# Block-recurrent attention and an ELU feed-forward on one core: batch 0 laid out as one hand-written order over all engines

## The chip, the cores and the metric

The kernel runs on one core of a Trainium2 chip. The metric is the device time of one execution in microseconds (us). Three runs of the kernel before gave 882.35 (median), 882.07 and 882.54 us.

A core has five engines that take instructions from queues of their own, in order, and hand results over by semaphores: PE (TensorE, matrix products and transposes), DVE (VectorE), ACT (ScalarE), POOL (GpSimd) and SP (SyncE, which here only issues DMAs). PEld is the loading of weights into PE.

## The reference, cut to what matters

Eight batches of 512 tokens; 8 heads of 64; each batch has 32 state rows per head.

```python
# x (8, 8, 512, 64) float32, state (8, 8, 32, 64) float32
# w_in (512, 2048), w_out (2048, 512): float64
scores = scale * x @ state.T                       # per batch and head
xread = softmax(scores) @ state                    # tokens read states
sread = softmax(scale * state @ x.T) @ x           # states read tokens
y = concat([xread, sread], axis=2)                 # (8, 8, 544, 64)
x = y.transpose(0, 2, 1, 3).reshape(8 * 544, 512)
h = x @ w_in
g = where(h > 0, h, exp(minimum(h, 0)) - 1)        # ELU
out = g @ w_out                                    # (4352, 512) float32
```

The softmaxes run over the last axis. Both weights arrive as float64, as pairs of 32-bit words, and the kernel makes float32 of them itself.

## The kernel before

**Batch by batch.** For each batch of 512 tokens the kernel does the attention, then 16 tiles of the hidden layer (`ffn1`, tile name `h_ps`, 128 hidden units by 512 tokens each) with the ELU on each, then the output layer (`ffn2`, `o_ps`) in four chunks of 128 tokens, each a sum over the 16 tiles. `xread` is never formed: `make_m` multiplies the transposed states (`kT`) with a quarter of `w_in` (512 columns) into `m_ps`, copied to `m_sb`, and `ffn1` multiplies that with the transposed attention weights `aT`. The state rows of all batches (`xT_state`) go through both layers at the end.

**Attention of a batch.** `turn_x` transposes x on PE in two halves (`xT_ps`), ACT copies them out; `by_state` gives the scores (`s_ps`, rows of 4 heads by 32 states; two halves g = 0, 1). `softmaxes` does both softmaxes for a half: over tokens by DVE (maximum, L221) and ACT (exp with sum, L229), over states by a 32x32 transpose on DVE (L226), maximum (L235), subtraction on POOL (L236), exp on ACT (L237), sum (L245), reciprocal and a multiplication on POOL (L250). `turn_tokens` transposes back to `aT` on DVE (L255), `turn_state` transposes `a_s` on PE, `state_read` computes `sr_ps`.

**The weights.** 32 pieces of 128x512: 16 of `w_in` (four column quarters of four pieces) and 16 of `w_out`. `load_weights` issues a transfer of 512 KB from SP into one of seven buffers named `raw`; `convert` turns the float64 words into float32 with three instructions on ACT (L150, L153, L156) and four on DVE (L157, L163, L167, L171). A buffer is free for the next transfer when the last of these has read it.

**ELU (`elu`).** ACT takes exp of `h_ps` into `e_sb` (L297), DVE limits it to 1 (L298), and DVE takes max(e - 1, h) into `g_sb` (L300).

**What sets the order.** PE's instructions stay in the order in which the code is written. Those of the other engines are put in order by a scheduler, which follows the order of the code loosely and mixes independent steps. In batch 0 the code is: states and x loaded, first quarter of `w_in` converted, attention of batch 0, the first `m`, then the 16 hidden tiles, with one more piece of weights converted after each; then all remaining pieces (`more(len(rest))`), and only then the output layer. From batch 1 on, the attention of the next batch is hooked in between the matmuls of the output layer, every fourth one, and the next `m` before the last chunk.

**PSUM.** `ps_a` is one buffer of two banks for all transposes, scores, `m_ps` and `sr_ps`; `ps_h` has three banks for `h_ps`; `ps_o` three for `o_ps`.

Of the kernel before, what the change touches and what calls it, by code (L numbers as in the profile page):

```python
# [25 lines left out]
def kernel(  # L26
# [23 lines left out]
    NB = S // 32  # L50
    scale = 1.0 / math.sqrt(D)
# [20 lines left out]
    rawpool = pool("raw", 7)  # L72
# [12 lines left out]
    def matmul(*args, **kw):  # L85
        tc.keep_in_program_order(nc.tensor.matmul(*args, **kw))  # L86

    def transpose(out, in_):
        tc.keep_in_program_order(nc.tensor.transpose(out, in_, ident))  # L89
# [8 lines left out]
    kT = cpool.tile([P, NP, B * NS], FP32, name="kT")  # L98
# [13 lines left out]
    def load_states():  # L112
        s_v = state.rearrange("(q b) (m c) n d -> q c b n m d", q=2, c=2)
        raw = [
            rawpool.tile([P, NP, P], FP32, tag="raw", name="s_sb").rearrange(
                "p m (c d) -> p m c d", c=2
            )
            for q in range(2)
        ]
        for q in range(2):  # L120
            for b in range(B // 2):
                for c in range(2):
                    (nc.sync, nc.scalar)[q].dma_start(
                        out=raw[q][b * NS : (b + 1) * NS, :, c], in_=s_v[q, c, b]
                    )
        return raw

    def turn_states(raw):
        ps = banks([P, 2, NP, P], "k_ps")
        for q in range(2):  # L130
            for m in range(NP):
                transpose(ps[:, q, m], raw[q][:, m].rearrange("p c d -> p (c d)"))
        nc.vector.tensor_copy(
            out=kT.rearrange("p m (q s) -> p q m s", q=2), in_=ps
        )

    def load_weights(src):
        k = src.shape[-1]
        raw = rawpool.tile([P, 512], moe_w_in.dtype, tag="raw", name="raw")
        nc.sync.dma_start(out=raw.rearrange("p (j k) -> p j k", k=k), in_=src)  # L140
        return raw

    def convert(dst, raw):
# [3 lines left out]
        words = raw.bitcast(U32).rearrange("p (j w) -> p j w", w=2)  # L147
        lo, hi = words[:, :, 0], words[:, :, 1]

        nc.scalar.activation(  # L150
            out=lo.bitcast(FP32), in_=lo, func=AF.Copy, scale=2.0**-29, bias=2.0**23
        )
        nc.scalar.activation(out=lo, in_=lo.bitcast(FP32), func=AF.Copy, bias=-(2.0**23))  # L153


        nc.scalar.activation(out=dst, in_=hi.bitcast(FP32), func=AF.Abs)  # L156
        nc.vector.tensor_scalar(  # L157
# [5 lines left out]
        nc.vector.tensor_scalar(  # L163
# [3 lines left out]
        nc.vector.scalar_tensor_tensor(  # L167
# [3 lines left out]
        nc.vector.tensor_tensor(out=bits, in0=bits, in1=lo, op=ALU.add)  # L171

    def load_w_in(c, n):
        cols = slice(c * 512, (c + 1) * 512)
        raw = load_weights(w_in_v[:, n : n + 1, cols])
        return lambda: convert(w_in[:, n, cols], raw)

    def load_w_out(fo):
        raw = load_weights(w_out_v[:, fo : fo + 1])
        return lambda: convert(w_out[:, fo], raw)  # L180

    def turn_x(b, i):

        ps = banks([P, 2, R, P], "xT_ps")
        for j in range(2):
            for r in range(R):
                m = 2 * i + j
                transpose(ps[:, j, r], x_t[b][:, r, m * P : (m + 1) * P])
        xT = xtpool.tile([P, 2, R * P], FP32, name="xT")
        for j in range(2):  # L190
            st[b, 2 * i + j] = xT[:, j]
            nc.scalar.copy(out=xT[:, j], in_=ps[:, j].rearrange("p r q -> p (r q)"))  # L192

    def by_state(b, name, rhs):
# [3 lines left out]
        for m in range(NP):  # L198
            for g in range(G):
# [3 lines left out]
                    kT[d, m, b * NS : (b + 1) * NS],  # L203
# [7 lines left out]
    def scores(b):  # L211

        ps = by_state(b, "s_ps", [st[b, m] for m in range(NP)])
        for g in range(G):
            softmaxes(b, g, ps[:, g])

    def softmaxes(b, g, ps):

        top = small.tile([P, 1], FP32, name="top")
        total = small.tile([P, 1], FP32, name="total")  # L220
        nc.vector.reduce_max(top, ps, axis=AX_X)  # L221
        nc.vector.tensor_scalar(
            out=top, in0=top, scalar1=-scale, scalar2=None, op0=ALU.mult
        )
        t = apool.tile([P, NB, NS], FP32, name="t_sb")
# [223 lines left out]
```

## Time and profile before

| | us |
|---|---|
| median of 3 runs (lowest, highest) | 882.35 (882.07, 882.54) |
| the profiled execution | 884.56 |
| its span, first to last instruction | 882.8 |
| PE busy in the span | 838.0 |
| DVE busy | 323.8 |
| ACT busy | 214.0 |
| POOL busy | 35.8 |

Times in the views are counted from the start of the span, and 1.8 us of the profiled execution lie outside it. A row of the timeline is: start, duration, engine, line, operation, tile written <- tiles read, shape, count, and in brackets how long the engine sat idle before it and what ended that. One float32 matmul of the program gives two MATMUL records on PE. Most lines of PE read L86 or L89, the helpers `matmul` and `transpose`; there one goes by tile names.

### The profile page before, as it was taken

How to read it: one execution, taken by the hardware profiler on the slowest of the kernel's cores; microseconds unless marked ns; L12 is line 12 of the kernel's file. 1: busy time of each engine (PE TensorE's matmuls, PEld its weight loads, DVE VectorE, ACT ScalarE, POOL GpSimd, SP SyncE). 2: the span in 40 equal slices, each digit the busy share in tenths (PEclk: the TensorE clock that was granted, in tenths of full speed). 3: DMA queues.
4: the chain of work that ended last, by engine and by line, in shares of the span. 5: the costliest groups of instructions: out<-in, count | busy, mean ns of one | idle time of the engine just before them, and what ended most of it. 6: DMA issues, size and time to landing. Idle time of an engine off the chain costs nothing.

```text
span 882.8 us, 7236 instructions
## 1 busy us (share of the span) xinstructions
PE 838.0 (95%) x2824; PEld 391.5 (44%) x2824; DVE 323.8 (37%) x658; ACT 214.0 (24%) x386; POOL 35.8 (4%) x38
## 2 busy tenths in 40 slices
PE   3487979999999999999999999999999999999997
PEld 2242435444543454445444454445434544444763
DVE  2869980263105340444026301632053403500220
ACT  4757730132003210222013201321033102200110
POOL 0200010001000010001000100001000100000000
PEclk9999989999999999999999999999999999999999
DMA  8564502100300011000200030000000000000000
GB/s 256 149 177 155 184 9 48 48 1 1 71 1 25 0 36 36 25 0 1 72 24 1 1 71 25 0 1 25 0 25 0 1 25 24 1 0 25 24 1 24
DMA packets 42914, 35.07 MB, mean 40 GB/s; under 512 B 36480, under 2 KB 36480, under 8 KB 42880
## 3 DMA queue, kind: packets, MB, share of 16 engines
q1 hardware_dynamic: 39648, 33.82, 12.9%
q10 hardware_dynamic: 3232, 0.79, 0.4%
q8 instruction: 22, 0.36, 0.2%
q14 instruction: 12, 0.10, 0.0%
HBM read 25.69 MB, written 8.91 MB: 39 GB/s over the span
## 4 chain that ended last, share of the span: by engine, by line
PE 89%; DVE 6%; DMA 2%; ACT 2%; issue 1%; POOL 0%; SPq 0%; ACTq 0%
PE o_ps L86 51%; PE h_ps L86 28%; PE sr_ps L86 4%; PE m_ps L86 3%; PE xT_ps L89 1%; DMA raw<-in_moe_w_in_dram 1%; DVE w_out L167 1%; PE sT_ps L89 1%; PE s_ps L86 1%; DVE w_out L171 1%; DVE w_out L157 1%; DVE g_sb L300 0%; DVE w_out L163 0%; DVE w_in L167 0%; DMA x_sb<-in_x_dram 0%
## 5 line engine op out<-in xcount | busy, mean ns | idle before, releaser
L86 PE MATMUL o_ps<-w_out,g_sb 128*128 128x512 f32 x1088 | 478.6, 595 | 0.0
L86 PEld LDWEIGHTS o_ps<-w_out,g_sb 128*128 128x128 f32 x1088 | 204.1, 191 | 252.3 <-issue 249.3
L86 PE MATMUL h_ps<-aT,m_sb 128*128 128x512 f32 x512 | 235.3, 613 | 9.7 <-ACT m_sb L291 6.4
L86 PEld LDWEIGHTS h_ps<-aT,m_sb 128*128 128x128 f32 x512 | 97.6, 195 | 146.0 <-issue 105.0
L297 ACT ACTIVATE e_sb<-h_ps 128x512 f32<-128x512 f32 (+1 forms) x144 | 82.5, 573 | 247.7 <-PE h_ps L86 247.6
L298 DVE TENSOR_SCALAR e_sb<-e_sb 128x512 f32<-128x512 f32 (+1 forms) x144 | 59.3, 412 | 104.2 <-ACT e_sb L297 104.0
L300 DVE SCALAR_TENSOR_TENSOR g_sb<-e_sb,h_ps 128x512 f32<-128x512 f32 (+1 forms) x144 | 94.6, 657 | 4.5
L347 DVE COPY o_sb<-o_ps 128x512 f32<-128x512 f32 x17 | 11.7, 691 | 175.4 <-PE o_ps L86 175.4
L291 DVE COPY m_sb<-m_ps 128x512 f32<-128x512 f32 x32 | 22.1, 690 | 116.7 <-ACT m_sb L291 116.7
L347 ACT COPY o_sb<-o_ps 128x512 f32<-128x512 f32 x17 | 9.8, 579 | 216.0 <-PE o_ps L86 216.0
L86 PE MATMUL m_ps<-w_in,kT 64*32 64x512 f32 x512 | 39.5, 615 | 10.7 <-ACT a_s L229 7.4
L236 POOL TENSOR_TENSOR t_sb<-t_sb,top_t 128x512 f32<-128x512 f32 x16 | 16.9, 1059 | 645.0 <-DVE top_t L235 518.1
L221 DVE TENSOR_REDUCE top<-s_ps 128x1 f32<-128x512 f32 x16 | 11.0, 685 | 68.2 <-PE s_ps L86 68.2
L86 PEld LDWEIGHTS sr_ps<-aT_s,x_sb 128*128 128x128 f32 x256 | 33.0, 209 | 4.9 <-issue 3.3
L86 PE MATMUL sr_ps<-aT_s,x_sb 128*128 128x64 f32 x256 | 32.9, 292 | 1.2 <-ACT aT_s L265 1.2
L291 ACT COPY m_sb<-m_ps 128x512 f32<-128x512 f32 x32 | 18.7, 585 | 42.7 <-PE m_ps L86 42.7
L86 PE MATMUL h_ps<-xT_state,w_in 128*128 128x256 f32 x128 | 27.8, 379 | 0.0
L192 ACT COPY xT<-xT_ps 128x512 f32<-128x512 f32 x32 | 17.1, 588 | 43.6 <-PE xT_ps L89 43.6
L86 PEld LDWEIGHTS h_ps<-xT_state,w_in 128*128 128x128 f32 x128 | 24.3, 190 | 3.7 <-issue 0.5
L150 ACT ACTIVATE raw<-raw 128x512 f32<-128x512 uint32 x32 | 21.8, 680 | 12.9 <-DMA raw<-in_moe_w_in_dram 9.2
L86 PEld LDWEIGHTS m_ps<-w_in,kT 64*32 64x32 f32 x512 | 6.2, 105 | 39.4 <-issue 23.5
L281 DVE COPY xT_state<-sr_ps 64x128 f32<-64x128 f32 x16 | 4.6, 289 | 51.0 <-PE sr_ps L86 50.9
(42 smaller groups left out, 306.1 us busy)
## 6 DMA issues: line engine op xcount, KB each, us to landing
raw<-in_moe_w_in_dram SPq DMA_DIRECT2D x16, 512.0 KB, 5.0
raw<-in_moe_w_out_dram SPq DMA_DIRECT2D x16, 512.0 KB, 3.3
out_dram<-o_sb SPq DMA_DIRECT2D x16, 512.0 KB, 2.6
x_sb<-in_x_dram SPq DMA_DIRECT2D x30, 256.0 KB, 4.3
x_sb<-in_x_dram ACTq DMA_DIRECT2D x2, 256.0 KB, 4.7
out_dram<-o_sb SPq DMA_DIRECT2D x8, 64.0 KB, 1.7
s_sb<-in_state_dram SPq DMA_DIRECT2D x8, 32.0 KB, 2.1
s_sb<-in_state_dram ACTq DMA_DIRECT2D x8, 32.0 KB, 3.1
```

What stands on the lines that cost most here:

```text
L86: tc.keep_in_program_order(nc.tensor.matmul(*args, **kw))
L89: tc.keep_in_program_order(nc.tensor.transpose(out, in_, ident))
L150: nc.scalar.activation(out=lo.bitcast(FP32), in_=lo, func=AF.Copy, scale=2.0**-29, bias=2.0**23)
L157: nc.vector.tensor_scalar(out=dst, in0=dst, scalar1=as_float(896 << 20), scalar2=as_float((1151 << 20) - 1), op0=ALU.max, op1=ALU.min,)
L192: nc.scalar.copy(out=xT[:, j], in_=ps[:, j].rearrange("p r q -> p (r q)"))
L221: nc.vector.reduce_max(top, ps, axis=AX_X)
L236: nc.gpsimd.tensor_tensor(out=t, in0=t, in1=bc(top_t, NS), op=ALU.subtract)
L291: (nc.scalar.copy, nc.vector.tensor_copy)[g % 2](out=m_t[b, c][:, g], in_=ps[:, g])
L297: nc.scalar.activation(out=e, in_=ps, func=AF.Exp)
L298: nc.vector.tensor_scalar(out=e, in0=e, scalar1=1.0, scalar2=None, op0=ALU.min)
L300: nc.vector.scalar_tensor_tensor(out=g[fo], in0=e, scalar=-1.0, in1=ps, op0=ALU.add, op1=ALU.max)
L347: (nc.scalar.copy, nc.vector.tensor_copy)[c % 2](out=o_sb[c // 2][:, c % 2], in_=o_ps)
```

## The change

Batch 0 is taken out of the loop and written as one function, `first_batch`. All engines but PE, which was so already, get an order that is fixed by the code for batch 0 (and SP for the whole kernel): a class `InOrder` wraps each engine and marks its instructions to stay in program order. A table of some 230 steps names each step of batch 0: `w:k.1` and `w:k.2` are the ACT part and the DVE part of converting piece k, `F:k` the hidden tile k, `R:k` its ACT part of the ELU, `E:k` its DVE part, `O:k` the output layer's share of tile k for all four chunks, `M` and `Mc` an `m` and its copies, `sc` the scores, `mx tr ae tm ps te su pm tt sd` the softmax steps, `sT sTc sr src` the state read, `x xc` the transposes of x and their copies.

- **Quarters.** The pieces come in the order: a quarter of `w_in`, then for each following quarter of `w_in` the quarter of `w_out` ahead of it, so that tile k can be taken through the output layer as soon as its piece of `w_out` is there. All four chunks accumulate through the whole of batch 0; the fourth bank is one of `ps_h`, which leaves two for `h_ps`.
- **Batch 1's attention** stands between the last tiles of batch 0; its first `m` (`M:1.0`) is the last PE step, and its copies follow it.
- **States.** One buffer of raw states in 8 transfers of 64 KB from SP, behind the transfer of piece 0; x of batch 0 comes in four transfers from ACT. `kT` is laid out by batch, and x of batch 1 is loaded behind piece 27, x of batch 2 behind the stores of batch 0.
- **ELU in all batches:** ACT computes relu(-h) and then exp(-that), DVE max(e - 1, h). DVE's limit to 1 goes.
- In batch 0 both copies of an `m` are on ACT.

The diff's core (the functions that only moved into named steps are left out):

```diff
+    class InOrder:
+        def __getattr__(self, name):
+            def call(*args, **kw):
+                ins = getattr(self.engine, name)(*args, **kw)
+                return tc.keep_in_program_order(ins) if self.on else ins
+            return call
...
     def load_states():
-        s_v = state.rearrange("(q b) (m c) n d -> q c b n m d", q=2, c=2)
-        for q in range(2):
-            for b in range(B // 2):
-                for c in range(2):
-                    (nc.sync, nc.scalar)[q].dma_start(
-                        out=raw[q][b * NS : (b + 1) * NS, :, c], in_=s_v[q, c, b]
-                    )
+        s_v = state.rearrange("b (m c) n d -> m c n b d", c=G)
+        for m in range(NP):
+            for c in range(G):
+                sync.dma_start(out=raw[m * NS : (m + 1) * NS, :, c], in_=s_v[m, c])
...
-        nc.scalar.activation(out=e, in_=ps, func=AF.Exp)
-        nc.vector.tensor_scalar(out=e, in0=e, scalar1=1.0, scalar2=None, op0=ALU.min)
+        scalar.activation(out=e, in_=ps, func=AF.Relu, scale=-1.0)
+        scalar.activation(out=e, in_=e, func=AF.Exp, scale=-1.0)
...
+    def first_batch():
+        plan = """
+            w:0.1 w:0.2 kT kTc x:0.0 xc:0.0 w:1.1 x:0.1 xc:0.1 w:1.2 w:2.1 sc:0 mx:0.0 w:3.1 w:2.2
...
+            O:4 w:19.2 R:5 w:20.2 w:21.1 F:6 w:22.1 E:5 M:0.2 w:17.2 R:6 F:7 Mc:0.2 w:22.2 w:23.1
...
+        order = [lambda n=n: load_w_in(0, n) for n in range(NP)]
+        for c in range(1, FC + 1):
+            if c < FC:
+                order += [lambda c=c, n=n: load_w_in(c, n) for n in range(NP)]
+            order += [lambda fo=fo: load_w_out(fo) for fo in range(4 * c - 4, 4 * c)]
...
+        load_x(0, [scalar])
+        fetch()
+        raw_states = load_states()
+        for k in range(NRAW - 2):
+            fetch()
...
+            elif name == "w":
+                (convert_1, convert_2)[num[1] - 1](*w[num[0]])
+                if num[1] == 2:
+                    fetch()
...
+    first_batch()
+    load_x(2, [sync])
+    for e in (vector, scalar, gpsimd):
+        e.on = False
+    for b in range(1, B):
+        batch(b)
+    states()
```

What this does to the order shows on PE, in the hidden layer of batch 0 (`h_ps`: hidden tiles, two matmuls each; `o_ps`: the output layer). Before:

```order
L86 MATMUL h_ps<-aT,m_sb 128x512 x8
L86 MATMUL m_ps<-w_in,kT 32x512 x8
L86 MATMUL h_ps<-aT,m_sb 128x512 x8
L86 MATMUL o_ps<-w_out,g_sb 128x512 x4
L89 MATMUL xT_ps<-ident,x_sb 128x128 x8
```

And now, from the first hidden tile on:

```order
L93 MATMUL h_ps<-aT,m_sb 128x512 x6
L93 MATMUL o_ps<-w_out,g_sb 128x512 x4
L93 MATMUL m_ps<-w_in,kT 32x512 x8
L93 MATMUL o_ps<-w_out,g_sb 128x512 x4
L93 MATMUL h_ps<-aT,m_sb 128x512 x2
L93 MATMUL o_ps<-w_out,g_sb 128x512 x4
```

The output layer's matmuls have moved up from behind all 16 hidden tiles to right behind the tile that they use.

On DVE, the conversions (`w_in<-raw`, `w_out<-raw`) before, in the middle of the hidden layer, with the ELU's steps (`e_sb`, `g_sb`) between them:

```order
L298 TENSOR_SCALAR e_sb<-e_sb 128x512
L157 TENSOR_SCALAR w_out<-w_out 128x512
L300 SCALAR_TENSOR_TENSOR g_sb<-e_sb,h_ps 128x512
L163 TENSOR_SCALAR w_out<-w_out 128x512
L298 TENSOR_SCALAR e_sb<-e_sb 128x512
L167 SCALAR_TENSOR_TENSOR w_out<-raw,w_out 128x512
```

And now, around the ELU of hidden tile 6 (`g_sb`), ahead of it piece 22, behind it piece 18:

```order
L93 TENSOR_SCALAR w_in<-w_in 128x512 x2
L93 SCALAR_TENSOR_TENSOR w_in<-raw,w_in 128x512
L93 ISA w_in<-raw,w_in 128x1024
L93 SCALAR_TENSOR_TENSOR g_sb<-e_sb,h_ps 128x512
L93 TENSOR_SCALAR w_out<-w_out 128x512 x2
L93 SCALAR_TENSOR_TENSOR w_out<-raw,w_out 128x512
L93 ISA w_out<-raw,w_out 128x1024
```

The four steps of one piece, each of which needs the one ahead of it, used to be mixed with those of another piece or of the ELU and now follow each other directly; the limiting step of the ELU (L298) is gone. On ACT the copies of the transposed x of batch 0 stand between whole pieces, so that ACT can't go on to piece 1 until the first half of x is transposed:

```order
L93 ACTIVATE raw<-raw 128x512 x2
L93 ACTIVATE w_in<-raw 128x512
L93 COPY xT<-xT_ps 128x512 x2
L93 ACTIVATE raw<-raw 128x512 x2
L93 ACTIVATE w_in<-raw 128x512
L93 COPY xT<-xT_ps 128x512 x2
```

Before, it went so:

```order
L150 ACTIVATE raw<-raw 128x512
L192 COPY xT<-xT_ps 128x512 x2
L153 ACTIVATE raw<-raw 128x512
L156 ACTIVATE w_in<-raw 128x512
L150 ACTIVATE raw<-raw 128x512
L192 COPY xT<-xT_ps 128x512 x2
```

The copies have moved from inside the conversion of a piece to behind it, and stay as early as they were.

361 lines of the change are left out of this document (221 added, 140 removed).

## The prediction

> **What bounds the kernel now.** I read the page's slices of busy time first, then the busy time by stage, then the chain of waits.
>
> ```profile
> PE   3487979999999999999999999999999999999997
> 0.00:48.90 48.90, 23.18 (x97) 13.89 (x98) 24.92 (x52) 27.21 (x49) 5.48 (x10) 1.00 0.66 194
> 48.90:97.60 48.70, 38.99 (x113) 14.67 (x113) 42.79 (x89) 33.99 (x60) 0.00 (x0) 0.89 0.56 173
> 97.60:168.94 71.34, 66.52 (x218) 31.93 (x217) 33.67 (x75) 19.69 (x36) 4.33 (x4) 0.95 0.21 59
> 168.94:263.63 94.69, 94.69 (x330) 43.03 (x329) 31.34 (x62) 18.99 (x34) 4.33 (x4) 1.00 0.09 23
> ```
>
> The first row is PE's busy share in slices of 22 us: idle time lies in the first seven (and at the very end). The others are stages (stretch, length, then busy us of PE, weight load, DVE, ACT and POOL, clock, DMA). Batch 1, from 168.94 to 263.63, has PE busy for all of its 94.69 us. The batches behind it look the same, so nothing that is done for DVE or ACT there can shorten them. The change can win only in batch 0, the 168.94 us before. There, the hidden layer (48.9 to 97.6) has DVE busy for 42.79 of 48.70 us and PE for 38.99, partly at a low clock (0.89).
>
> ```profile
> 168.94 3.43 PE h_ps L86 x8
> 173.40 7.06 PE h_ps L86 x16
> 180.46 1.02 PE m_ps L86 x16
> 200.06 3.43 PE o_ps L86 x8
> 203.50 0.88 PE xT_ps L89 x8
> 212.11 1.02 PE s_ps L86 x16
> 223.63 0.88 PE sT_ps L89 x8
> 227.94 3.52 PE sr_ps L86 x32
> ```
>
> These rows of the chain (start, duration, what, records) are prices of PE at full clock: a hidden tile 7.06 / 4 = 1.77 us (between the starts 168.94 and 200.06, with three m taken off, 1.75), the output layer's share of a tile 3.43, an m or the scores 1.02, eight transposes 0.88, a state read 3.52. Batch 0 costs PE, with its own attention and that of batch 1, about 16 x (1.75 + 3.43) + 5 m + 2 x (1.02 + 2 x 0.88 + 0.88 + 3.52) + 0.9 for kT = 103 us. It takes 168.94 us. So up to 60 us lie open, less what the start must cost.
>
> **The new batch 0 as a sum.** The order is now fixed on every engine, so I look for the engine that comes last at each meeting of PE and DVE, and add: (a) until the scores are there, (b) DVE's queue from there to the last point at which PE waits for it, (c) PE's work from that point on.
>
> (a) The start.
>
> ```profile
> 0.74 3.19 DMA x_sb<-in_x_dram
> s_sb<-in_state_dram SPq DMA_DIRECT2D x8, 32.0 KB, 2.1
> 7.58 1.09 PE L89 MATMUL k_ps<-ident,s_sb 128*128 128x128 f32 x4 [7.58 <-DMA s_sb<-in_state_dram]
> 9.39 1.11 PE L89 MATMUL k_ps<-ident,s_sb 128*128 128x128 f32 x4 [0.72 <-DMA s_sb<-in_state_dram]
> 10.55 1.23 DVE L133 COPY kT<-k_ps 128x1024 f32<-128x1024 f32 x1 [10.55 <-PE k_ps L89]
> 18.81 1.96 PE L86 MATMUL s_ps<-xT,kT 64*32 64x512 f32 x16 [1.16 <-ACT xT L192]
> ```
>
> Before, the second half of the raw states is there at 9.39, kT's copy starts at 10.55, and the scores end at 18.81 + 1.96 = 20.8, so the copy-to-scores chain is 10.2 us (transposes and copies that wait for each other; the change keeps it). Now the states go behind piece 0 and beside all of x, and the built program makes the last of their eight transfers wait for the third quarter of x to land. One quarter of x took 3.19 us from its issue at 0.74 to 3.93; three in a row land at 8 by that, and a state transfer takes 2.1 more. All eight transposes then follow (1.09 + 1.11). So they start between 9.0 (fewer transfers ahead, nothing earlier than before is likely) and 10.1; I take 9.5. The scores end at 9.5 + 2.2 + 10.2 = 21.9. Piece 0 converts earlier than now, but that is not on the path: the DVE step behind it waits for the scores.
>
> (b) DVE from the first maximum (`mx:0.0`) up to piece 18 (`w:18.2`), which is the last thing that the output share of tile 6 waits for.
>
> ```profile
> 16.77 0.43 DVE L157 TENSOR_SCALAR w_in<-w_in 128x512 f32<-128x512 f32 x1 [5.00 <-ACT w_in L156]
> 17.23 0.43 DVE L163 TENSOR_SCALAR w_in<-w_in 128x512 uint32<-128x512 uint32 x1
> 17.69 0.69 DVE L167 SCALAR_TENSOR_TENSOR w_in<-raw,w_in 128x512 uint32<-128x512 uint32 x1
> 18.42 0.69 DVE L171 CUSTOM_DVE_ANT_0 w_in<-raw,w_in 128x1024 uint16<-128x1024 uint16 x1
> 118.62 0.68 DVE L171 CUSTOM_DVE_ANT_0 w_out<-raw,w_out 128x1024 uint16<-128x1024 uint16 x1
> 119.22 0.68 DVE L167 SCALAR_TENSOR_TENSOR w_out<-raw,w_out 128x512 uint32<-128x512 uint32 x1
> L300 DVE SCALAR_TENSOR_TENSOR g_sb<-e_sb,h_ps 128x512 f32<-128x512 f32 x128 | 87.9, 687 | 3.9
> L298 DVE TENSOR_SCALAR e_sb<-e_sb 128x512 f32<-128x512 f32 x128 | 54.6, 427 | 88.1 <-ACT e_sb L297 87.9
> L226 DVE STREAM_TRANSPOSE t_sb<-s_ps 128x512 f32<-128x512 f32 x16 | 11.2, 701 | 0.0
> L222 DVE TENSOR_SCALAR top<-top 128x1 f32<-128x1 f32 x16 | 2.1, 129 | 0.0
> L249 DVE RECIPROCAL total_t<-total_t 128x16 f32<-128x16 f32 x16 | 4.0, 252 | 0.5
> ```
>
> The first four rows are one piece whose steps follow each other directly, as all pieces do now: starts 0.46, 0.46 and 0.73 apart. An independent instruction follows after 0.60 (118.62 to 119.22, although each lasts 0.68). A piece thus takes 0.46 + 0.46 + 0.73 + 0.60 = 2.25 us of DVE; mixed with others, as before, it took about 2 x 0.34 + 2 x 0.60 = 1.88. This is what the fixed order costs. By the plan, 20 pieces (2, 3, 4, 6, 8, 7, 5, 9, 10, 12, 13, 11, 15, 16, 14, 19, 20, 17, 22, 18) stand in this stretch: 45.0. Seven ELU steps at 0.60: 4.2. Softmax of batch 0: ten long passes (maxima, transposes, sums, transposes back) at 0.63 (0.70 less the overlap of some 0.08), eight short ones between 0.13 and 0.25 and one scaling at the 0.43 of L298: 8.2. Sum 57.4. The limiting step that is removed from ELU spares seven times 0.34 here, 2.4 us.
>
> ACT must keep ahead.
>
> ```profile
> L150 ACT ACTIVATE raw<-raw 128x512 f32<-128x512 uint32 x32 | 21.8, 680 | 12.9 <-DMA raw<-in_moe_w_in_dram 9.2 <-DMA raw<-in_moe_w_out_dram 3.5 <-DVE w_out L157 0.2
> L297 ACT ACTIVATE e_sb<-h_ps 128x512 f32<-128x512 f32 x128 | 76.4, 597 | 212.7 <-PE h_ps L86 212.5
> L291 ACT COPY m_sb<-m_ps 128x512 f32<-128x512 f32 x32 | 18.7, 585 | 42.7 <-PE m_ps L86 42.7
> ```
>
> From the second copy of x (about 20 us) until the ELU of tile 6 it has 21 pieces at no more than 3 x 0.68, seven ELUs at 2 x 0.60, four copies of m and four exps at about 0.6: 56 us at the most, so to 76. DVE needs that ELU at 21.9 + 57.4 - 2.85 = 76.5. It fits, with little to spare; by starts instead of durations ACT has some 5 us less.
>
> At the ScalarE: Activation LUTs page (rules for kernel authors) the Trainium skill says to put relu on VectorE and not on ScalarE, which speaks against this ELU. The rows agree on the price of one (0.597 against 0.427), but by that rule the sum would be 2.4 us longer, since here DVE comes last and ACT does not.
>
> POOL stands in DVE's way:
>
> ```profile
> 28.43 1.23 POOL L250 TENSOR_TENSOR t_sb<-t_sb,total_t 128x512 f32<-128x512 f32 x1
> 28.75 1.19 DVE L157 TENSOR_SCALAR w_in<-w_in 128x512 f32<-128x512 f32 x1
> 32.25 1.30 POOL L250 TENSOR_TENSOR t_sb<-t_sb,total_t 128x512 f32<-128x512 f32 x1 [2.59 <-DVE total_t L249]
> 32.58 1.53 DVE L167 SCALAR_TENSOR_TENSOR w_in<-raw,w_in 128x512 uint32<-128x512 uint32 x1
> ```
>
> Two conversions that began during a POOL pass took 1.19 for 0.43 and 1.53 for 0.69. Four POOL passes lie in stretch (b), each beside a piece; between 0 and 4 x 0.8; I take three, 2.4. The Trainium skill, SBUF — State Buffer (who interferes with whom), calls this an exclusive lock held for a whole instruction; by it all four would block DVE, up to 1.23 each, and the sum would be 2.5 us longer.
>
> (c) PE from the output share of tile 6 to the first tile of batch 1: ten shares (34.3), tiles 9 to 15 (12.3), two m, sc, two sT, two x, two sr (2.0 + 1.0 + 1.8 + 1.8 + 7.0): 60.2. By DVE's tally tiles 12 to 15 and the attention of batch 1 need nothing that comes later than PE gets there. The last m is now directly ahead of batch 1, with its copy uncovered: 0.6 for ACT's half plus hand-overs, 0.8.
>
> Hand-overs and misfits in (b), between 0 and 3: the first two hidden tiles come from a cold PE, and the ELU behind them is wanted by DVE only 0.7 us after my tally has it; I take 1.5.
>
> Sum: 21.9 + 57.4 + 2.4 + 1.5 + 60.2 + 0.8 = 144.2 against 168.94, a gain of 24.7. The profiled execution took 884.56, so 859.9; the median of 882.35, 2.2 lower, becomes 857.7.
>
> **What I cost at nothing.** ELU in batches 1 to 7 and the states: ACT has 18.99 of 94.69 us there, and PE needs a bank back only after two more tiles (3.5 us), while relu, exp and the last DVE step take 0.60 + 0.60 + 0.69 and hand-overs, about 2.0. The transfers of the weights:
>
> ```profile
> DMA to landing us min/median/max: 3.0/4.0/10.4
> ```
>
> That is for `raw`. A buffer is refilled when DVE lets go of it, and by the tallies ACT wants the new piece 6 us later or more; 4.0 fits.
>
> **Rivals.**
>
> - *The longer ELU bounds batches 1 to 7 (slower).* If relu, exp and DVE's step with their waits took more than two tiles (3.5 us), PE would wait at every tile. 24.7 us spread over 128 tiles is 0.19 each, so from 3.7 us on the change loses; at 3.9 it gives 857.7 + 128 x 0.4 = 909 or so. Against it: the 2.0 above, and no row that comes near. Chance 0.04, of which 0.03 slower.
> - *PE falls to a low clock in the lockstep with DVE.*
>
> ```profile
> 74.01 1.13 PE L86 MATMUL h_ps<-aT,m_sb 128*128 128x512 f32 x2 [2.24 <-ACT m_sb L291]
> 76.54 7.95 PE L86 MATMUL h_ps<-aT,m_sb 128*128 128x512 f32 x14 [1.41 <-DVE m_sb L291]
> ```
>
> After waits of 2.24 and 1.41 us, 14 matmuls took 7.95, where 7.06 x 14 / 16 = 6.2 is the full-clock time: 1.8 lost. With six such losses up to tile 6, or between shares behind it, 11 us: 869. Against it: my waits there are under 1.3 us. Chance 0.08. (TensorE: Matmul & The Clock Gate, on its second failure mode, says in the Trainium skill that frequent micro-idles do this; the clock of 0.89 in the hidden layer agrees, for longer waits.)
> - *Late transfers block the ordered queues.* If pieces took the worst landing of 10.4 against 6.1 us of room, ACT, and DVE and PE behind it, would wait 4.3 us in each of three rounds of the seven buffers: 13 us, 871. Only the first loads, issued all at once, were that late. Chance 0.06.
> - *DVE is faster than I sum.* Without the POOL collisions and with pieces at 1.88, F:0 comes 1.5 earlier and behind it PE itself is at most 2.7 us behind DVE: 2.4 + 4.2 = 6.6 less, 851. Chance 0.10.
>
> **How the numbers follow.** My case has 0.72. Its own range, from the start (1 each way), POOL (-2.4 to +2.5), misfits (-1.5 to +1.5) and 0.1 per piece (2), is 852 to 865. To hold 8 in 10 with the rivals of a smaller and a larger gain it goes from 850 to 869. A measurement of this kernel can tell about 0.2%, 1.8 us, from no change. Every case but the first rival gains more than that: faster 0.96, same 0.01, slower 0.03.
>
> **What would show it.** Right: scores end near 22; the first hidden tile starts near 40; the output share of tile 6 waits for DVE's last step of piece 18 near 83, and from there PE has no wait but the 0.8; batch 1 starts near 144 and has 94.7 us again; DVE is close to full between 22 and 83. Wrong: PE waits behind tile 6, ACT waits for `raw`, PE waits in batch 1, or the start of batch 1 lies beyond 157 or before 137.

## The result: 862.47 us, and the profile after

| | before | after |
|---|---|---|
| median (lowest, highest), us | 882.44 (882.07, 882.85; 4 runs) | 862.47 (862.37, 862.76; 4 runs) |
| profiled execution, its span | 884.56, 882.8 | 862.39, 860.6 |
| start of batch 1 | 168.94 | 146.45 |
| from there to the end of the span | 713.86 | 714.15 |
| busy PE, DVE, ACT | 838.0, 323.8, 214.0 | 823.3, 275.8, 303.1 |

The ratio is 0.9774 (95% interval 0.9757 to 0.9791), so the change is faster by 20.0 us. All of it lies ahead of batch 1. Behind it nothing changed, although ACT has two passes in each ELU now.

The slices of busy time of the kernel after, 21.5 us each:

```profile
PE   2299999999999999999999999999999999999997
DVE  1999944423033401432032402440042303300110
PEclk9889999999999999999999999999999999999999
```

PE was at 3, 4, 8, 7, 9, 7 before. Now only the first two slices show it idle. DVE is at 9 in slices 2 to 5. The busy time by stage (stretch, length, then busy us and instructions of PE, weight load, DVE, ACT and POOL, clock, DMA share, GB/s), cut at the first maximum, at the output share of tile 6 and at batch 1:

```profile
0.00:24.53 24.53, 7.84 (x40) 4.94 (x40) 5.71 (x10) 9.19 (x15) 0.71 (x6) 1.00 0.90 235
24.53:85.09 60.56, 45.29 (x132) 17.52 (x133) 58.02 (x107) 54.41 (x94) 4.42 (x4) 0.92 0.52 172
85.09:146.45 61.36, 60.62 (x253) 31.16 (x252) 38.41 (x79) 30.86 (x55) 4.34 (x4) 1.00 0.17 53
146.45:241.10 94.65, 94.65 (x328) 43.13 (x329) 26.19 (x48) 29.60 (x52) 4.33 (x4) 1.00 0.17 39
```

The first three rows are the three terms of the sum. In the second row DVE is busy for 58.02 of 60.56 us and ACT for 54.41. In the third PE is busy for all but 0.74 us. The fourth is batch 1, as full as before.

The start, in the timeline of after:

```profile
0.74 5.76 ACTq L93 DMA_DIRECT2D x_sb<-in_x_dram  x4
1.19 9.16 SPq L93 DMA_DIRECT2D s_sb<-in_state_dram  x8
12.94 1.94 PE L93 MATMUL k_ps<-ident,s_sb 128*128 128x128 f32 x8 [12.94 <-DMA s_sb<-in_state_dram]
22.46 1.96 PE L93 MATMUL s_ps<-xT,kT 64*32 64x512 f32 x16 [1.16 <-ACT xT L93]
24.53 0.69 DVE L93 TENSOR_REDUCE top<-s_ps 128x1 f32<-128x512 f32 x1 [1.04 <-PE s_ps L93]
```

SP was still issuing state transfers at 10.35, and the state transposes could start only at 12.94. The chain of waits says why: the last state transfer waits for a quarter of x to land.

```profile
1.86 8.16 DMA x_sb<-in_x_dram
10.04 2.55 DMA s_sb<-in_state_dram
```

In the stretch behind the first maximum POOL and DVE meet:

```profile
30.16 1.60 DVE L93 TENSOR_SCALAR w_in<-w_in 128x512 f32<-128x512 f32 x2
30.32 1.15 POOL L93 TENSOR_TENSOR t_sb<-t_sb,top_t 128x512 f32<-128x512 f32 x1 [29.01 <-DVE top_t L93]
38.46 0.65 DVE L93 TENSOR_SCALAR total_t<-total_t 128x16 f32<-128x16 f32 x1
39.31 1.56 DVE L93 TENSOR_SCALAR w_in<-w_in 128x512 f32<-128x512 f32 x2
```

The first two steps of a conversion take 0.88 together without POOL. Here they take 1.60, at 33.73 again 1.61, and 1.56. The small 128x16 instruction takes 0.17 elsewhere and 0.65 here. Together that is 0.72 + 0.73 + 0.48 + 0.68 = 2.6 us. And the meeting of PE and DVE, with the last step of piece 18:

```profile
43.09 8.05 PE L93 MATMUL h_ps<-aT,m_sb 128*128 128x512 f32 x12 [8.03 <-DVE aT L93]
79.84 3.70 PE L93 MATMUL o_ps<-w_out,g_sb 128*128 128x512 f32 x8 [0.27 <-DVE w_out L93]
84.20 0.69 DVE L93 CUSTOM_DVE_ANT_0 w_out<-raw,w_out 128x1024 uint16<-128x1024 uint16 x1
85.09 3.60 PE L93 MATMUL o_ps<-w_out,g_sb 128*128 128x512 f32 x8
146.45 3.70 PE L93 MATMUL h_ps<-aT,m_sb 128*128 128x512 f32 x8 [0.74 <-ACT m_sb L93]
```

The first hidden tile waits for DVE's token transpose until 43.09. The share of tile 5 still waits 0.27 for piece 17. The share of tile 6 starts at 85.09, as soon as PE is there, 0.2 us behind the end of piece 18; PE has no wait at this point. From there PE only waits for the copy of batch 1's first m, 0.74.

### The profile page after: what moved, and what is told of

Read it like the earlier page. It is cut to its first block, busy times and chain, and to the rows that moved or that the text cites. A ratio compares the mean times of both kernels' runs of the same rounds, so it can differ in the third digit from the quotient of the medians.

```text
span 860.6 us, 7230 instructions
## 1 busy us (share of the span) xinstructions
PE 823.3 (96%) x2824; PEld 385.0 (45%) x2824; DVE 275.8 (32%) x510; ACT 303.1 (35%) x534; POOL 35.5 (4%) x38
## 3 DMA queue, kind: packets, MB, share of 16 engines
q10 hardware_dynamic: 4160, 1.05, 0.7%
## 4 chain that ended last, share of the span: by engine, by line
PE 91%; DVE 6%; DMA 2%; ACT 0%; issue 0%; ACTq 0%; SPq 0%
PE o_ps L93 53%; PE h_ps L93 28%; PE m_ps L93 3%; PE sr_ps L93 3%; DVE w_in L93 3%; PE xT_ps L93 2%; DVE w_out L93 2%; PE s_ps L93 1%; DMA x_sb<-in_x_dram 1%; PE sT_ps L93 1%; DMA raw<-in_moe_w_in_dram 0%; DVE g_sb L93 0%; DMA s_sb<-in_state_dram 0%; DVE total_t L93 0%; ACT xT L93 0%
## 5 line engine op out<-in xcount | busy, mean ns | idle before, releaser
L93 PE MATMUL h_ps<-aT,m_sb 128*128 128x512 f32 x512 | 231.7, 603 | 9.0 <-DVE aT L93 8.0
L93 ACT ACTIVATE e_sb<-e_sb 128x512 f32<-128x512 f32 (+1 forms) x144 | 87.5, 608 | 4.6
L93 DVE COPY m_sb<-m_ps 128x512 f32<-128x512 f32 x28 | 19.2, 686 | 113.7 <-ACT m_sb L93 113.7
L93 PE MATMUL m_ps<-w_in,kT 64*32 64x512 f32 x512 | 37.5, 615 | 6.9 <-ACT a_s L93 6.8
L93 ACT ACTIVATE raw<-raw 128x512 f32<-128x512 uint32 x64 | 43.6, 681 | 1.0
L93 PEld LDWEIGHTS sr_ps<-aT_s,x_sb 128*128 128x128 f32 x256 | 29.8, 192 | 3.8 <-issue 3.6
L93 PE MATMUL sr_ps<-aT_s,x_sb 128*128 128x64 f32 x256 | 29.4, 273 | 0.0
L93 ACT ACTIVATE a_s<-s_ps,top 128x512 f32<-128x512 f32 x16 | 11.0, 689 | 34.7 <-DVE top L93 29.4
```

The source lines that it names most:

```text
L93: ins = getattr(self.engine, name)(*args, **kw)
```

## The experiments

Theory at the outset: the gain is what the sum says, and three things hold it back: states that land late, POOL's collisions, and the directly chained steps of the fixed order. The table holds the marks of all variants of the kernel after, in us of their profiled executions. The last column is the whole time (median of four).

| kernel | states there | first maximum | first hidden tile | share of tile 6 | batch 1 | time |
|---|---|---|---|---|---|---|
| after | 12.94 | 24.53 | 43.09 | 85.09 | 146.45 | 862.47 |
| states first | 10.74 | 26.46 | 45.02 | 87.03 | 148.39 | 864.18 |
| old ELU | 13.85 | 25.43 | 43.99 | 88.70 | 150.17 | 865.89 |
| no fixed order | 13.22 | 26.05 | 37.31 | 77.59 | 138.96 | 854.80 |
| no POOL passes | 12.94 | 24.53 | 40.42 | 82.27 | 143.63 | 860.00 |
| softmax first | 13.59 | 25.18 | 38.52 | 85.48 | 146.84 | 862.86 |
| pairs | 13.14 | 24.73 | 43.28 | 85.30 | 146.66 | 863.23 |
| both edits | 13.28 | 24.86 | 38.18 | 83.80 | 145.16 | 861.23 |
| DVE free | 13.48 | 25.18 | 38.85 | 81.89 | 143.25 | 859.46 |
| ACT free | 13.46 | 25.97 | 44.82 | 88.32 | 149.80 | 866.12 |
| x first, no fixed order | 14.80 | 20.70 | 34.65 | 75.52 | 136.88 | 852.92 |
| states and x first, no fixed order | 12.30 | 17.30 | 33.12 | 73.47 | 134.93 | 851.08 |

("States there" is the start of their transposes; in the last two rows these stand behind the transposes of x, so the states may have landed earlier.) From batch 1 to the end of the span every one of them took between 714.07 and 714.16 us, so a difference in the column of batch 1 is a difference of the whole. Beside the experiments the kernel before had medians of 883.55 to 884.27, and all its runs, the first ones too, lie between 881.83 and 885.34.

**States first.**

```diff
+        raw_states = load_states()
         load_x(0, [scalar])
         fetch()
-        raw_states = load_states()
```

> The changed kernel with the eight state transfers issued ahead of the first piece and of x. Theory 1 (the states are late because they stand behind piece 0 and behind x): the state transposes start about as early as before the change, near 9 instead of 12.9, the first maximum comes 3 to 5 us earlier than 24.53, and the whole gains as much: 857 to 860 against 862.5. Rival (the engines of the DMA are bound by the volume of x, states and first pieces, so that an order only decides which of the two is late): then x lands later by what the states land earlier, the first maximum stays within 1 us of 24.5, and the time is 861.5 to 863.5.

864.18 us, 1.7 slower: neither theory. The states were there 2.2 us earlier, but the timeline shows who held them up then:

```profile
10.74 1.94 PE L93 MATMUL k_ps<-ident,s_sb 128*128 128x128 f32 x8 [10.74 <-DMA s_sb<-in_state_dram]
12.68 1.33 ACT L93 ACTIVATE raw<-raw 128x512 f32<-128x512 uint32 x2 [6.73 <-DMA raw<-in_moe_w_in_dram]
16.25 0.69 DVE L93 CUSTOM_DVE_ANT_0 w_in<-raw,w_in 128x1024 uint16<-128x1024 uint16 x1
16.86 1.22 DVE L93 COPY kT<-k_ps 128x1024 f32<-128x1024 f32 x1
```

Piece 0 now lands last, at 12.68, and in the fixed order DVE converts it ahead of kT's copy. PE had the transposes done at 12.68; their copy starts at 16.86. The rival's volume argument is borne out by the DMA's rate in slices of 0.65 us (of the same kernel):

```profile
DMA  0016999999999999899999999999999510000000
GB/s 0 0 32 149 285 262 210 218 197 212 218 216 217 204 202 170 227 366 429 397 359 403 422 416 403 334 384 403 435 416 391 214 57 25 0 0 0 0 0 0
```

The engines of the DMA are full from 2.6 us on. While x and states flow, in packets under 512 bytes, they move some 210 GB/s, and behind them, with the pieces alone, some 400.

**The old ELU.** The edit puts the exp and DVE's limit to 1 back.

```diff
-        scalar.activation(out=e, in_=ps, func=AF.Relu, scale=-1.0)
-        scalar.activation(out=e, in_=e, func=AF.Exp, scale=-1.0)
+        scalar.activation(out=e, in_=ps, func=AF.Exp)
...
+        vector.tensor_scalar(out=e, in0=e, scalar1=1.0, scalar2=None, op0=ALU.min)
```

> The changed kernel with the ELU as it was (exp on ACT, limit to 1 on DVE, then max(e - 1, h)). Theory 1 (DVE comes last in the stretch from the first maximum to piece 18): seven limiting steps of 0.34 to 0.46 stand there again, 2.4 to 3.2 us, so batch 1 starts near 149 instead of 146.45 and the time is 864.5 to 866. Rival (ACT is the bound or as close, so that two passes on ACT cost what one on DVE spares, as a rule of taking relu off ACT would have it): 862.5 or less. Outside batch 0 neither expects a difference, since PE is full there.

865.89 us, 3.4 slower, as theory 1 has it. In the profiled execution the states come 0.9 later, which is not the ELU's doing; from the first maximum to the share of tile 6 it took 63.27 us against 60.56, which is 2.71 for seven steps. PE's timeline shows where they come up:

```profile
80.88 1.98 PE L93 MATMUL h_ps<-aT,m_sb 128*128 128x512 f32 x4 [2.17 <-DVE g_sb L93]
88.70 3.70 PE L93 MATMUL o_ps<-w_out,g_sb 128*128 128x512 f32 x8
```

**The new ELU alone, in the kernel before.** The same two lines, the other way round.

> The kernel before with nothing but the new ELU. Theory 1 (the ELU is worth only what it takes off DVE in batch 0; batches 1 to 7 are full on PE): 16 tiles at 0.34 are 5.4 us at most, and waits for other things take part of it: 877 to 882.4 and batches 1 to 7 unchanged at 94.7 us. Rival (the ELU gave the greater part of the 20 us, as a shorter queue of DVE lets everything move up): 872 or less.

877.26 us: a ratio of 0.9927 (0.9912 to 0.9942) to the 884.07 of before at its side, 5.1 to 7.8 us. Theory 1 held: batch 1 starts at 161.45, over 7 us ahead of the profiled run of before, and behind it nothing moves. It is a little more than the 5.4 of DVE's steps; the 16 hidden tiles with their three m end 5.6 us earlier, some of them run at a higher clock than before (14 records in 6.50 instead of 7.97), and what is gained beyond that comes and goes with single waits (a wait of 4.68 us for batch 1's `a_s` is gone, one of 3.85 for its `xT` is new).

**No fixed order.** The steps, quarters and transfers stay; only DVE, ACT and POOL are left to the scheduler.

```diff
+    for e in (vector, scalar, gpsimd):
+        e.on = False
     first_batch()
     load_x(2, [sync])
-    for e in (vector, scalar, gpsimd):
-        e.on = False
```

> The changed kernel with its steps, quarters and transfers as they are, but with the order on DVE, ACT and POOL in batch 0 left to the scheduler, which mixes independent steps (four DVE steps of a piece cost 1.88 us when mixed, 2.25 when they follow each other directly). Theory 1 (the gain comes from the output layer's shares between the hidden tiles, not from the exact order; the order costs 0.37 for each of 20 pieces and avoids misplaced steps): within 8 us of 862.5 to either side, and PE still goes to the shares right behind the hidden tiles. Rival (the order worked out step by step is what brings it): 870 or more, with long waits of PE for steps that the scheduler has put behind conversions which nobody awaits yet.

854.80 us, 7.7 faster than the change. Theory 1 held, and what the fixed order does is to lose time. The stages of this kernel, cut at its first maximum, first hidden tile and batch 1:

```profile
0.00:26.05 26.05, 7.84 (x40) 4.93 (x40) 10.77 (x19) 12.47 (x21) 0.70 (x6) 1.00 0.95 260
26.05:37.31 11.26, 1.96 (x16) 0.25 (x17) 11.12 (x21) 10.72 (x23) 5.18 (x4) 1.00 0.28 96
37.31:138.96 101.65, 100.90 (x369) 48.03 (x369) 71.88 (x156) 67.53 (x123) 4.44 (x5) 1.00 0.38 120
```

Though its first maximum comes 1.5 us later, it needs 11.26 us from there to the first hidden tile, where the change needs 18.56; and from that tile on PE has no wait but the last 0.74, so the third row, 101.65, is the least that PE took for this stretch in any run; the change needs 103.36. (Of it the first three tiles take 6.95, where three later ones take 5.2.) In the first row DVE has 19 instructions behind it where the change has 10: the scheduler converts pieces while DVE would wait for the scores, and behind the scores it puts the softmax ahead of the conversions.

The next four runs ask which part of that is worth what.

**No POOL passes.**

```diff
     def row_subtract(b, g):
+        if b == 0:
+            return
...
     def row_scale(b, g):
+        if b == 0:
+            return
```

> The changed kernel without the four POOL passes of batch 0 (the subtraction of the row maximum and the multiplication by the reciprocal are left out, so batch 0's attention weights over states are not normalised). Theory 1 (POOL's passes stretch four steps of DVE by 2.6 us in all, and DVE is what the first hidden tile and the share of tile 6 wait for): first hidden tile and batch 1 start 2.5 to 3.5 us earlier (the wait for the second pass itself goes too): 859 to 860. Rival (PE is the bound from the first hidden tile on, and the chain through ACT and the first m sets that tile): under 1 us, 861.5 or more.

860.00 us. The first maximum is unchanged to the hundredth, and the first hidden tile, the share of tile 6 and batch 1 come 2.67, 2.82 and 2.82 earlier: theory 1. (That is 0.2 more than the stretched steps add up to; the passes themselves are gone from the chain as well.) The first two steps of the conversion at 30.16 last 0.87 now:

```profile
30.16 0.87 DVE L93 TENSOR_SCALAR w_in<-w_in 128x512 f32<-128x512 f32 x2
37.00 0.17 DVE L93 TENSOR_SCALAR total_t<-total_t 128x16 f32<-128x16 f32 x1
40.42 6.89 PE L93 MATMUL h_ps<-aT,m_sb 128*128 128x512 f32 x12 [5.97 <-DVE aT L93]
```

**Softmax first.** `w:4.2` and `w:6.2` move from between the softmax steps to behind `tt:0.1`.

```diff
-            w:6.1 w:4.2 ps:0.1 te:0.1 su:0.0 Mc:0.0 su:0.1 pm:0.0 w:8.1 w:6.2 pm:0.1 w:9.1 tt:0.0
-            w:7.1 tt:0.1 w:8.2 F:0 w:10.1 F:1 w:7.2 R:0 w:11.1 E:0 w:5.2 F:2 R:1 O:0 R:2 E:1 w:9.2
+            w:6.1 ps:0.1 te:0.1 su:0.0 Mc:0.0 su:0.1 pm:0.0 w:8.1 pm:0.1 w:9.1 tt:0.0
+            w:7.1 tt:0.1 w:4.2 w:8.2 F:0 w:6.2 w:10.1 F:1 w:7.2 R:0 w:11.1 E:0 w:5.2 F:2 R:1 O:0 R:2 E:1 w:9.2
```

> The changed kernel with the DVE steps of pieces 4 and 6 moved from between the softmax steps to behind the last token transpose; each piece still in one go. The kernel without the fixed order started its first hidden tile at 37.31 instead of 43.09 and PE never waited after. Theory 1 (two bounds lie within 2 us of each other: PE from its first hidden tile on, 101.7 us to batch 1, and DVE's queue up to piece 18, which this doesn't shorten): the first hidden tile starts 4 to 5 us earlier, at 38 to 39, but the share of tile 6 still starts at 84 to 85 and batch 1 at 145.5 to 146.5: 861.5 to 862.6. Rival (the late first tile alone is the loss): batch 1 4 to 5 us earlier, 858.

862.86 us, as theory 1 has it. The first hidden tile starts at 38.52, 4.6 us earlier, and all of it is given back to DVE's queue, as PE's timeline shows:

```profile
38.52 8.12 PE L93 MATMUL h_ps<-aT,m_sb 128*128 128x512 f32 x12 [2.68 <-DVE aT L93]
49.37 3.70 PE L93 MATMUL o_ps<-w_out,g_sb 128*128 128x512 f32 x8 [2.73 <-DVE g_sb L93]
77.98 1.98 PE L93 MATMUL h_ps<-aT,m_sb 128*128 128x512 f32 x4 [1.60 <-DVE g_sb L93]
```

**Pairs.** DVE's four steps of two pieces alternate, six times from piece 8 on: 8 and 7, 10 and 12, 13 and 11, 15 and 16, 19 and 20, 17 and 22.

```diff
+    def convert_2(*pairs):
+        steps = [convert_steps(*p) for p in pairs]
+        for fs in zip(*steps):
+            for f in fs:
+                f()
```

> The changed kernel with twelve of the pieces behind the first hidden tile converted in pairs, DVE's four steps of one piece alternating with those of the other (1.88 us a piece by the start-to-start times, instead of 2.25). Theory 1 (two bounds): DVE is 12 x 0.37 = 4.5 us earlier at piece 18, but the first hidden tile stays at 43.1 and PE's 101.7 us follow it: batch 1 at 144.7 to 145.3, 860.7 to 861.4. Rival (DVE's queue alone is the loss): batch 1 near 142, 858.

863.23 us, no gain. Theory 1 is right in that DVE's queue alone wasn't the loss, but the 1.1 to 1.8 us that it expected didn't come either. PE ran up to tile 7 without a wait and then had one for the pair that holds piece 17, whose steps are now delayed by those of piece 22 and by ACT, which brings piece 22 late:

```profile
80.04 3.70 PE L93 MATMUL o_ps<-w_out,g_sb 128*128 128x512 f32 x8 [1.73 <-DVE w_out L93]
```

**Both edits,** with 4 and 8, 6 and 7 as pairs.

> Both edits together, with pieces 4 and 8, 6 and 7 as pairs too (seven pairs). Theory 1 (two bounds, each of which hides the other): the first hidden tile at 38 to 39, piece 18 some 5 us earlier, batch 1 at 140 to 141 and 856 to 857.5, about 6 us less, though neither edit alone gives 2; most of the 7.7 us that the kernel without the fixed order is faster is then explained by these two. Rival (the scheduler wins by ACT's order or by the transfers): 859 or more.

861.23 us: the first tile at 38.18 as expected, but batch 1 only at 145.16. By the expectation's terms that is the rival: something else is close behind. The pairs themselves work (DVE's timeline, pieces 10 and 12, and the first step behind them):

```profile
53.13 0.42 DVE L93 TENSOR_SCALAR w_out<-w_out 128x512 f32<-128x512 f32 x1
53.46 0.42 DVE L93 TENSOR_SCALAR w_in<-w_in 128x512 f32<-128x512 f32 x1
...
56.28 0.68 DVE L93 CUSTOM_DVE_ANT_0 w_in<-raw,w_in 128x1024 uint16<-128x1024 uint16 x1
56.88 0.42 DVE L93 TENSOR_SCALAR w_in<-w_in 128x512 f32<-128x512 f32 x1
...
70.72 0.43 DVE L93 TENSOR_SCALAR w_in<-w_in 128x512 f32<-128x512 f32 x1 [1.13 <-ACT w_in L93]
```

Two pieces take 56.88 - 53.13 = 3.75, 1.87 each. But now DVE waits for ACT (1.13 at piece 20, 0.44 at piece 22), which has no gap left. In the changed kernel ACT's two dependent steps stand next to each other; without the fixed order the independent one stands between them. ACT in the timeline of after:

```profile
67.29 1.38 ACT L93 ACTIVATE raw<-raw 128x512 f32<-128x512 uint32 x2
68.58 0.65 ACT L93 ACTIVATE w_out<-raw 128x512 f32<-128x512 f32 x1
69.13 1.40 ACT L93 ACTIVATE raw<-raw 128x512 f32<-128x512 uint32 x2
```

And in the kernel without the fixed order:

```profile
58.22 0.68 ACT L93 ACTIVATE raw<-raw 128x512 f32<-128x512 uint32 x1
58.79 0.66 ACT L93 ACTIVATE w_out<-raw 128x512 f32<-128x512 f32 x1
59.36 1.25 ACT L93 ACTIVATE raw<-raw 128x512 uint32<-128x512 f32 x2
```

A piece takes 69.13 - 67.29 = 1.84 in the one and three starts 0.57 apart, 1.71, in the other.

**DVE free, and ACT free.** Two runs with the scheduler on one engine only; the first has

```diff
+    for e in (vector,):
+        e.on = False
     first_batch()
     load_x(2, [sync])
-    for e in (vector, scalar, gpsimd):
+    for e in (scalar, gpsimd):
```

and the second the same with `scalar`.

> The changed kernel with the order left to the scheduler on DVE alone; ACT and POOL keep the fixed order of batch 0. Theory 1 (DVE's order brings most of the 7.7 us: softmax steps ahead of conversions, and steps of two pieces mixed): first hidden tile at 37.5 to 38.5, batch 1 at 140 to 141.5, 856 to 858. Rival (ACT is a third bound just behind the other two: in the paired kernel it was busy for 34.2 of 35.6 us, its three steps of a piece 1.85 us when they follow each other against 1.68 when mixed, so 20 pieces cost it 3.4 us): the first hidden tile is early, but DVE waits for ACT before the share of tile 6, batch 1 at 143 to 146, 859 to 862.

> The changed kernel with the order left to the scheduler on ACT alone; DVE and POOL keep the fixed order of batch 0. With DVE's order free alone the time was 859.46, with all three free 854.80, so ACT's order was worth 4.7 us once DVE's was free. Theory 1 (the queues stand side by side, and what is gained on one is hidden behind the next: DVE's fixed queue up to piece 18 still ends at 84 to 85): batch 1 at 145.5 to 146.5, 861.5 to 862.6. Rival (ACT's order is worth its 4.7 us by itself, the effects add up): 857 to 858.5.

DVE free: 859.46, in the rival's range, but not for its reason. DVE hardly waited for ACT. The first hidden tile began at 38.85 and its second matmul could follow only at 41.94, when the other half of the token transpose was there:

```profile
38.85 2.05 PE L93 MATMUL h_ps<-aT,m_sb 128*128 128x512 f32 x2 [2.72 <-DVE total_t L93]
41.94 6.77 PE L93 MATMUL h_ps<-aT,m_sb 128*128 128x512 f32 x10 [1.04 <-DVE aT L93]
```

From then on PE had no wait until batch 1's first m. So what is left against the kernel without the fixed order lies ahead of that point. There the first m waited 1.32 us for piece 3, and the softmax's exps stood behind whole pieces on ACT. That ACT's order is what this cost is a reading of the trace: POOL's order was fixed here too, and no run frees DVE and ACT without POOL.

ACT free: 866.12, 3.6 slower than the change; both theories missed. The scheduler puts conversions ahead of steps that others wait for, and ACT then sits at pieces that haven't landed. What ACT waited for up to 90 us:

```profile
ACT raw L93 <- DMA raw<-in_moe_w_in_dram: 15.6, 6, 6.4
```

Two effects reach the others: the first maximum comes 1.4 us later (0.5 of it from the states, 0.9 from the first copy of x, which ACT now does behind pieces), and DVE waits 1.47 for the ELU of tile 0. How much more of the 15.6 us counts is not shown. So what the orders are worth can't be added up: DVE alone free gains 3.2 at batch 1, ACT alone loses 3.4, and all three free gain 7.5.

**A version that beats both.** Two runs on the kernel without the fixed order. In the first, x of batch 0 is transposed ahead of the states, in banks of the hidden layer that are free then:

```diff
-        ps = banks([P, 2, R, P], "xT_ps")
+        if b:
+            ps = banks([P, 2, R, P], "xT_ps")
+            ps = [ps[:, j] for j in range(2)]
+        else:
+            ps = [ps_h.tile([P, R, P], FP32, tag="h", name="xT_ps") for j in range(2)]
...
-            w:0.1 w:0.2 kT kTc x:0.0 xc:0.0 w:1.1 x:0.1 xc:0.1 w:1.2 w:2.1 sc:0
+            w:0.1 w:0.2 x:0.0 xc:0.0 x:0.1 xc:0.1 kT kTc w:1.1 w:1.2 w:2.1 sc:0
```

> The kernel without the fixed order on DVE, ACT and POOL, with x of batch 0 transposed ahead of the states, into the two free banks of the hidden layer instead of the one buffer that all transposes share; the states' transfers stay behind piece 0. Theory 1 (the start is a chain of transposes and copies behind the last state transfer, 13.2 us, and x is there by about 8): the scores follow kT directly, first maximum at 18 to 20 instead of 26.05, first hidden tile 4 to 7 us earlier than 37.31, and the time 848 to 851 against 854.8. Rival (the first four pieces land and are converted no earlier, and the first m waits for piece 3): under 2 us gained, 853 to 855.

852.92 us, between the two. The first maximum comes at 20.70, 5.35 earlier, but the first hidden tile only 2.66, since the stretch between them grew from 11.26 to 13.95: there the pieces are the bound, for the chain of waits runs over a piece that lands at 18.45 and the conversions behind it. The second one issues the states' transfers first, as in the first experiment:

> The same, with the states' eight transfers issued ahead of piece 0 as well. Theory 1 (volume of small packets: x and states take the same time in any order, the pieces behind them then land at the full rate of some 400 GB/s): kT at about 12.7 instead of 15.2, piece 0 at 12.7 instead of 8.1 but piece 3 no later than before, first maximum at 16.5 to 18, 846 to 850. Rival (as with the fixed order, where states first gave nothing: what the states gain, the pieces lose, and ACT starts 4.5 us later with a queue that has little room): no better than the kernel with x first alone, or up to 3 us worse.

851.08 us (850.27 to 851.64; ratio to before 0.9628, 0.9612 to 0.9643), 11.4 under the change and 1.1 above the range that was expected. What lost 1.7 us in the fixed order, where kT stood behind piece 0, gains 1.8 here. Its stages, cut as those of the kernel without the fixed order:

```profile
0.00:17.30 17.30, 6.45 (x40) 4.45 (x40) 3.62 (x6) 7.80 (x13) 0.70 (x6) 1.00 1.02 258
17.30:33.12 15.82, 3.87 (x16) 0.43 (x17) 15.82 (x34) 15.67 (x31) 4.53 (x4) 0.56 0.60 213
33.12:134.93 101.81, 101.06 (x369) 47.75 (x369) 73.11 (x158) 67.74 (x122) 4.43 (x5) 0.98 0.38 120
```

Now DVE and ACT are full between the first maximum and the first hidden tile (15.82 and 15.67 of 15.82 us), and the DMA is full ahead of it. From the first tile on PE is at its minimum again.

## Why the prediction was right, and where it was off

The forecast was 857.7 with a range of 850 to 869; 862.47 lies 4.8 above it. The mechanism was the one predicted in the main: between the first maximum and the share of tile 6 DVE is the fullest engine (58.02 of 60.56 us), PE waits for it, and behind that PE is full. But PE does not wait at the share of tile 6, though the prediction expected it to. Its last waits for DVE are 0.18 ahead of tile 7 and 0.27 for piece 17, and piece 18 is done 0.2 us before PE gets to it. There is a second bound that the sum does not have: PE itself, from its first hidden tile on. 43.09 + 101.65 = 144.74 is only 1.7 us less than the measured start of batch 1. More work on DVE still counts (2.71 in the run with the old ELU), less hardly does (no gain with pairs). That the path that was summed ties with this one is luck, and it let the sum come out. The terms:

| term | predicted | measured |
|---|---|---|
| (a) state transposes start | 9.5 (9.0 to 10.1) | 12.94 |
| (a) first maximum | 21.9 | 24.53 |
| (b) DVE to the share of tile 6 | 57.4 + 2.4 + 1.5 = 61.3 | 60.56 |
| in it: POOL collisions | 2.4 (0 to 3.2) | 2.6 |
| (c) PE to batch 1 | 60.2 + 0.8 = 61.0 | 61.36 |
| batch 1 | 144.2 | 146.45 |
| rest of the span | as before, 713.86 | 714.15 |

- **The step that failed is the start.** The prediction had three quarters of x land by 8 and the last state transfer behind them at the price of before, 2.1 us. The quarter of x that this transfer waits for took 8.16 us and landed at 10.0, the transfer took 2.55, and PE began 0.35 behind it: 12.94 where 9.5 was taken. From there to the first maximum it took 11.6 us where 2.2 + 10.2 = 12.4 were summed, so (a) is 2.6 late in all. What the term left out is volume: x (1.05 MB), the states (0.52) and piece 0 (0.52) all share DMA engines that move some 210 GB/s while such packets flow: 2.1 MB are 10 us, and with the 2.6 us until the engines are full, 12.6 by this estimate. States first showed that the same volume, ordered otherwise, only makes another transfer the late one; the states-and-x-first kernel showed that this is worth something once nothing in order stands behind the late one.
- **The base.** The sum was made against the profiled execution, 884.56, and shifted by the 2.2 us by which it lay above the median. After's profiled execution, 862.39, lies at its median. The gain is 22.2 by the spans and 20.0 by the medians, and the 2.2 between them was the scatter of the kernel before, whose runs spread over 3.5 us. With 2.25 from the start of batch 1 and 0.3 from the rest that is the 4.8. (Half of the 0.3 is only where one looks: the chain has batch 1 of before start at 168.94, the timeline at 168.78.)
- **(b) is right within 1 us**, by its parts: pieces at 2.25, ELU steps (2.71 for seven steps of the old one, 2.4 predicted), POOL. The Trainium skill's rule in SBUF — State Buffer (who interferes with whom), an exclusive lock for a whole instruction, agrees with the 1.60 and 1.56 for 0.88, and with their going when POOL's passes are left out; four passes at their full length, 2.5 us above the 2.4, did not come: each cost DVE 0.5 to 0.7 of its 1.05 to 1.16 us. The rows fit that DVE was in the middle of an instruction when the pass began (POOL's at 30.32, DVE's at 30.16).
- **The ELU in batches 1 to 7** cost nothing, as said: ACT is busy for 29.60 of 94.65 us instead of 18.99, and PE is full. The rule to keep relu off ACT (ScalarE: Activation LUTs, rules for kernel authors, in the Trainium skill) would have cost 2.7 us here, by the stretch up to the share of tile 6 in the run with the old ELU.
- **The low clock in lockstep** and **late transfers** didn't come up: from 50.97 to 85.09 the granted clock is 1.00, and ACT waits for no transfer between 24.53 and 85.09. The clock is 0.92 on average in the stretch because it is 0.50 from 39 to 47, at the end of the wait of 8.03 us and behind it; the 12 records of the first three tiles took 8.05 us (6.82 in the pairs kernel, at a clock of 1.00).
- **DVE faster than summed** (851) asked for pieces at 1.88 and no collisions. Neither is what the change does. The kernel without the fixed order, with pieces mixed, gained 7.5 where the rival named 6.6, but that the two are near is chance: its first tile comes 5.8 us earlier, which the rival had at 1.5, and its steps still meet POOL (at 29.76, 30.85 and 35.18 single steps take 1.17, 1.26 and 1.37 us). The prediction wrote "this is what the fixed order costs" beside the 2.25; that the order as a whole costs more than it brings was not said, and is what the runs show.

What stays open: how the 7.5 us divide between the mixing of steps and their place. At the start of batch 1, pairs and softmax first gained nothing alone and 1.3 together, DVE free gained 3.2, and ACT free lost 3.4.

## What to carry to other kernels

When three engines come within a few us of each other, as DVE, ACT and PE do in this batch, an edit on one shows only up to the next, and what edits are worth can't be added up (3.2 gained, 3.4 lost, and 7.5 gained with all three engines free): look for the least time that PE needs (101.65 here) and ask what keeps it from starting. Before an order is fixed by hand on an engine, run the same steps with the order left open, and fix only what that shows to be misplaced; in a fixed order keep independent steps between dependent ones, and put nothing that nobody awaits ahead of a step that another engine waits for. Price a first load by the bytes ahead of it on all queues, at the rate that such transfers reach together, and by the transfer that it waits for, not by what one transfer took when it had less beside it.

## What the runs showed of the hardware

- An instruction that needs the result of the one directly ahead of it on its engine starts later than an independent one. On DVE a piece takes 2.25 us when its four steps follow each other and 1.87 when they alternate with another's. On ACT it is 1.84 against 1.71. The Trainium skill, VectorE: DVE Perf Modes (The DRAIN you can't avoid), says of eight tensor_copies that a semaphore behind each cost nothing extra. Here a step that waits for the one directly ahead of it costs 0.1 us more than one that doesn't (0.46 and 0.33 from start to start), and the measurement decides.
- POOL's pass holds up even a 128x16 instruction of DVE, for 0.48 us (0.65 instead of 0.17).
- While x and the states flowed, in packets under 512 bytes, the DMA engines were full at some 210 GB/s; with the pieces alone, at some 400. No run changed the packets alone.
- The kernel before scattered over 3.5 us in 32 runs; the mean clock, on record for 28 of them, was 0.990 to 0.993. In the four runs of each kernel that the result rests on it scattered over 0.8 us and the kernel after over 0.4, at 0.994 to 0.999. No run was made to show what the scatter comes from.
